# Decode attention beside an MLP on one core: the K and V loads of a unit, cut in two and issued from two queues

## The chip, the cores and the metric

The kernel runs on one core of a Trainium2 chip. The metric is the time of one execution on the device in microseconds (us), as the median of three runs. Beside the timed runs there is one profiled execution, whose trace is what the text reads. Of the engines, PE multiplies matrices, DVE works on vectors, ACT computes activations, POOL does odd jobs, and SP only issues transfers. A transfer is issued as an instruction of an engine's own stream (here SP's or ACT's), waits there for what it needs, and then goes into that engine's queue. The bytes are moved by 16 DMA engines, on which each queue has its share of every transfer.

## The reference, cut to what matters

Two batches, one query token each, 32 heads of 128, a cache of 16384 keys and values per head, all in bf16:

```
q = (x @ wq)                      # x: 2 x 1 x 1024, wq: 1024 x 4096
p = softmax(q . k_cache^T * 128**-0.5)     # k_cache: 2 x 32 x 16384 x 128
a = (p . v_cache) @ wo            # v_cache as k_cache, wo: 4096 x 1024
x1 = x + shifted(gelu(layernorm(x) @ w1)) @ w2
b = x1 + gelu(layernorm(x1) @ w3) @ w4
g = sigmoid(sum(x * gate_w))
out = g * a + (1 - g) * b
```

With one token, the shift of the mixer brings in nothing but zeros. K and V together are 537 MB of some 573 MB read.

## The kernel before, in words

**Units.** The work of attention is cut into 32 units (L88): 16 pairs of heads by 2 batches. The K of a unit is 8.39 MB, laid on 128 partitions as rows of 256 x 128 bf16, so 64 KB in a partition; its V likewise. `cache_rows` (L90) gives that view of the cache, in which each row is contiguous.

**Memory.** One tile `mem` (L80) has five cells of 32 KB per partition. K of an even unit lies in cells 0 and 1, of an odd unit in cells 1 and 2 (`k_cell`, L85): two units in a row share cell 1. V lies in cells 3 and 4 (`v_cell`, L86), but V of unit 30 in 0 and 1. The weights borrow cells: wq lies in 3 and 4 at the start (L124), w1 and w2 in 2, w3 and w4 in 3 and 4 after that (L254 to L257). Whoever loads a cell waits until its last readers are done.

**Loads.** `load_k` and `load_v` (L96, L99) are one transfer each, from SP. `load_v_half` (L102) loads half a row and is used for V of unit 0 alone; `load_v_pieces` (L109) loads V of unit 31 in nine pieces. The weights, x and wo come from SP too (L125, L127, L226, L428, L436). ACT issues nothing but half of the output at the end (L680).

**A unit n** (the loop from L630):
1. `score_first(n)`: four chunks of the half of K that lies in cell 1. DVE transposes a chunk (L462, 2.3 us), then PE does eight matmuls of it into S (L468).
2. `load_k(n + 1)`, which has to wait until cell 1 is free, so for the fourth of these transposes.
3. `score_second(n)`: the other four chunks.
4. `softmax_a(n)`: a transpose (L489) and a maximum (L491) on DVE, a scaled identity `Dm` on ACT (L493).
5. `pv(n - 2)`: 64 matmuls of the V of two units ago (L543).
6. `load_v(n - 1)`, into the cells that these matmuls have read.
7. `pv_end(n - 2)` on DVE and PE, with `wo_project` (L441) in every second unit.
8. `softmax_b(n)`: a matmul (L499), a minimum on DVE (L505), two Exp on ACT (L507). `softmax_c(n)`: a matmul (L521) and a reciprocal (L523).

In unit 31 the V of unit 30 takes the place of step 2 (L635), and the nine pieces of V of unit 31 that of step 6 (L662). In every fourth unit `load_wo_pair` (L428) brings 1 MB of wo from SP. Units 0 and 1 have the MLP's second half (L640 to L656) in place of steps 5 to 7. Before the loop stand the q projection (L268), the gate, the layer norms and the MLP's first half (L623 to L628).

**Order.** Each engine runs its instructions in one order, and that of the source decides except where the framework puts an instruction forward: at 66.20 us matmuls of w3 (L233) run between those of the scores. Semaphore waits are added by the framework, which knows parts of a tile apart. ACT's instructions per unit are `Dm` and then the two Exp, nothing else.

The lines that the diff is about:

```
    def load_k(u):
        nc.sync.dma_start(out=region(k_cell[u], NJ * Dh), in_=cache_rows(A_k_cache, u))

    def load_v(u):
        nc.sync.dma_start(out=region(v_cell[u], NJ * Dh), in_=cache_rows(A_v_cache, u))
```

Of the kernel before, what the change touches and what calls it, by code (L numbers as in the profile page):

```python
# [23 lines left out]
def kernel(  # L24
# [15 lines left out]
    nc = tc.nc  # L40
    P = nc.NUM_PARTITIONS
    B, Sq, D = A_x.shape
    _, H, Sk, Dh = A_k_cache.shape
# [11 lines left out]
    NJ = 2 * Sk // P  # L55
# [6 lines left out]
    CELL = NJ * Dh // 2  # L62
# [19 lines left out]
    def region(cell, elements):  # L82
        return mem[:, cell * CELL : cell * CELL + elements]

    k_cell = [0 if u % 2 == 0 else 1 for u in range(NU)]  # L85
    v_cell = [3] * NU  # L86
# [3 lines left out]
    def cache_rows(cache, u):  # L90
        hp, b = units[u]
        return cache[b, 2 * hp : 2 * hp + 2].rearrange("h s d -> (h s) d").rearrange(
            "(p j) d -> p (j d)", p=P
        )

    def load_k(u):  # L96
        nc.sync.dma_start(out=region(k_cell[u], NJ * Dh), in_=cache_rows(A_k_cache, u))

    def load_v(u):  # L99
        nc.sync.dma_start(out=region(v_cell[u], NJ * Dh), in_=cache_rows(A_v_cache, u))  # L100

    def load_v_half(u, k):  # L102
        at = slice(k * CELL, (k + 1) * CELL)
# [17 lines left out]
    def v_view(u):  # L121
# [12 lines left out]
        out=ident_s[:], in0=ident_f[:], scalar1=-scale, scalar2=None, op0=ALU.mult  # L134
# [8 lines left out]
    for v in range(4):  # L143
        w, e = divmod(v, 2)
        nc.gpsimd.affine_select(
            out=sel[:, v],
            in_=sel[:, v],
# [9 lines left out]
        out=mask4[:], in_=mask4[:], compare_op=ALU.is_ge, fill=0.0,  # L157
# [3 lines left out]
        out=mask4[:], in_=mask4[:], compare_op=ALU.is_ge, fill=0.0,  # L161
# [10 lines left out]
        out=lmat[:].rearrange("p (g h k) -> p g h k", h=2, k=4),  # L172
        in_=hm2[:].unsqueeze(1).unsqueeze(3).to_broadcast([P, P // 8, 2, 4]),
# [4 lines left out]
        out=sel8[:],  # L178
        in_=ident_f[:].rearrange("p (c k) -> p k c", k=QP)[:, 0:8, :],
# [8 lines left out]
        out=hsel[:], in_=sel8[:].rearrange("p (h k) -> p h k", k=4), axis=AX.X, op=ALU.add  # L188
# [69 lines left out]
    lin1.load()  # L258
    lin2.load()
    load_k(0)  # L260

    xT = const.tile([P, KC, B], BF16)
# [27 lines left out]
    for e in range(2):  # L290
        rows = slice(e * HALF, (e + 1) * HALF)
        nc.vector.tensor_copy(
            out=qd[rows],
            in_=qdps[rows].rearrange("p v (hp e b) -> p hp e b v", e=2, b=B)[:, :, e],
# [335 lines left out]
    for n in range(NU):  # L630
        score_first(n)
        if n + 1 < NU:
            load_k(n + 1)
        else:
            load_v(NU - 2)  # L635
        score_second(n)
        softmax_a(n)
        if n == 0:
            load_wo_pair(0)
            lin3.compute(0, 0, FC // 2)  # L640
            softmax_b(n)
            lin3.compute(0, FC // 2, FC)
            lin4.load(0)
            softmax_c(n)
            lin3.compute(1, 0, FC)
            lin4.load(1)
            gelu_T(lin3.acc[:], h2T[:], FC)
        elif n == 1:
            lin4.compute(0, 0, KC // 2)
            softmax_b(n)  # L650
            lin4.compute(0, KC // 2, KC)
            load_v_half(0, 0)
            softmax_c(n)
            lin4.compute(1, 0, KC)
            load_v_half(0, 1)
            mlp_post4()  # L656
        else:
            pv(n - 2)
            if n < NU - 1:
                load_v(n - 1)  # L660
            else:
                load_v_pieces(NU - 1)  # L662
            pv_end(n - 2)
            if n == NU - 1:
                load_wo_last()
            softmax_b(n)
            softmax_c(n)
# [11 lines left out]
    for b, queue in ((0, nc.sync), (1, nc.scalar)):  # L679
        queue.dma_start(  # L680
            out=out[b, 0].rearrange("(k n) -> k n", k=Q4),
            in_=out_row[b : b + QP * (Q4 - 1) + 1 : QP, :],
# [31 lines left out]
```

## Time and profile before

| what | value |
|---|---|
| median of three runs | 1341.24 us (1341.04 to 1341.56) |
| the profiled execution | 1341.09 us |
| its span | 1339.4 us |
| PE, DVE, ACT busy | 768.8, 705.1, 105.2 us (57%, 53%, 8%) |
| bytes moved | 573.33 MB in 14486 packets, 428 GB/s on average |
| rate in the first, the middle and the last of 40 slices | 406, 435 or so, 309 GB/s |
| loads of K, from issue to landing | 28.2 us (25.8 to 30.8) |
| loads of V, from issue to landing | 33.2 us (17.3 to 35.9) |
| SP waiting with a K load in hand (L97) for DVE's transposes of cell 1 | 329.4 us in 31 waits |
| SP waiting with a V load in hand (L100) for PE's pv | 157.9 us in 29 waits |
| DVE waiting for K | 219.5 us in 30 waits |

The span runs from the first to the last instruction, and the time of an execution has 1.7 us more. The busy time of PE, DVE and ACT says how much of the span each works; what matters is who is waited for last. A wait of SP costs nothing as long as the DMA engines have other transfers in their queues; the page's row "DMA" tells how full these are. Queues go by number: q1 is SP's, q10 is ACT's, q8 brings instructions. A packet is one contiguous run of bytes on one DMA engine, here a row in one partition. Landing times are as the semaphores show them. All times on a timeline count from the span's start.

### The profile page before, as it was taken

Reading aid. Unit: us, or ns where it says so; the run is one execution under the profiler, and the core shown is the slowest. Engines: PE = TensorE matmul, PEld = TensorE weight load, DVE = VectorE, ACT = ScalarE, POOL = GpSimd, SP = SyncE. Lnnn points to the kernel's source line nnn. Section 1 sums busy time; section 2 is a strip of 40 time slices with the busy share of each in tenths; the row PEclk is TensorE's granted clock in tenths of the full one; section 3 lists DMA queues with packets and bytes.
Section 4 is the critical chain, followed back from the end, with each engine's and each line's share of the span. In section 5 each row is a group of like instructions: output and inputs, shape, how many; then the busy total and the mean of one; then the engine's idle time right before and its main releaser. Section 6 shows DMA issues by size and latency. Waiting matters only on the chain.

```text
span 1339.4 us, 12490 instructions
## 1 busy us (share of the span) xinstructions
PE 768.8 (57%) x5502; PEld 351.9 (26%) x5502; DVE 705.1 (53%) x695; ACT 105.2 (8%) x165; POOL 15.2 (1%) x54
## 2 busy tenths in 40 slices
PE   2688566554566645556654546665455665555564
PEld 2456222222222212222222212222122222222222
DVE  1445566554556554556655445656444665545561
ACT  0011000000000000000000000000000000000000
POOL 1000000000000000000000000000000000000000
PEclk9977887776788777788877778877678886777886
DMA  9999999999999999999999999999999999999997
GB/s 406 425 429 432 440 431 433 435 423 440 429 435 437 429 429 437 425 435 435 435 431 429 429 437 431 429 427 430 440 431 431 427 433 423 437 435 435 433 423 309
DMA packets 14486, 573.33 MB, mean 428 GB/s; under 512 B 1880, under 2 KB 1888, under 8 KB 4448
## 3 DMA queue, kind: packets, MB, share of 16 engines
q1 hardware_dynamic: 14424, 572.54, 99.3%
q8 instruction: 43, 0.70, 0.2%
q14 instruction: 11, 0.09, 0.0%
q10 hardware_dynamic: 8, 0.00, 0.0%
HBM read 572.53 MB, written 0.00 MB: 427 GB/s over the span
## 4 chain that ended last, share of the span: by engine, by line
DMA 67%; PE 16%; DVE 12%; issue 4%; ACT 0%; another core or an unknown queue 0%; POOL 0%; SPq 0%; ACTq 0%; DVEq 0%
DMA mem<-in_A_k_cache_dram 62%; PE S L468 12%; DVE KT L462 12%; PE misc L233 2%; DMA mem<-in_A_v_cache_dram 2%; DMA xin<-in_A_x_dram 2%; DMA wo<-in_A_wo_dram 1%; PE misc L268 1%; ACT pt L507 0%; PE arow L402 0%; PE oacc L543 0%; DVE St L489 0%; POOL ln_rstd L350 0%; PE misc L344 0%
## 5 line engine op out<-in xcount | busy, mean ns | idle before, releaser
L468 PE MATMUL S<-KT,qw 128*128 128x512 bf16 x2048 | 544.2, 415 | 369.5 <-DVE KT L462 369.3
L462 DVE STREAM_TRANSPOSE KT<-mem 128x2048 f32<-128x2048 f32 x256 | 570.9, 2283 | 271.7 <-DMA mem<-in_A_k_cache_dram 219.5
L468 PEld LDWEIGHTS <-qw 128*128 128x128 bf16 x2048 | 217.7, 107 | 688.3 <-issue 509.2
L543 PE MATMUL oacc<-mem,pt 128*8 128x512 bf16 x2008 | 116.9, 384 | 8.7 <-DMA mem<-in_A_v_cache_dram 8.7
L507 ACT ACTIVATE pt<-St,nb 64x256 bf16<-64x256 f32 x64 | 90.0, 1406 | 149.5 <-DVE nb L505 148.6
L493 ACT ACTIVATE Dm<-ident_s,m 128x128 f32<-128x128 f32 x32 | 12.8, 401 | 998.8 <-DVE m L491 998.8
L521 PE MATMUL misc<-rs,lmat 128*128 128x1 f32 x62 | 18.2, 362 | 85.8 <-ACT pt L507 85.6
L543 PEld LDWEIGHTS <-pt 128*8 128x8 bf16 x2008 | 46.4, 87 | 76.2 <-issue 25.9
L489 DVE STREAM_TRANSPOSE St<-S 128x512 f32<-128x512 f32 x32 | 22.9, 717 | 66.6 <-PE S L468 66.6
L523 DVE RECIPROCAL rinv<-misc 128x1 f32<-128x1 f32 x31 | 5.2, 169 | 96.3 <-PE misc L521 96.3
L559 DVE TENSOR_SCALAR part<-oacc,maskr 128x128 f32<-128x128 f32 x31 | 10.9, 351 | 83.0 <-PE oacc L543 83.0
L590 PE MATMUL misc<-hsel,red 128*128 128x2 f32 x112 | 17.5, 261 | 51.5 <-DVE red L565 51.5
L521 PEld LDWEIGHTS misc<-rs,lmat 128*128 128x128 f32 x62 | 15.5, 310 | 94.2 <-ACT pt L507 94.2
L233 PEld LDWEIGHTS <-mem 128*128 128x128 bf16 x576 | 36.9, 169 | 2.2 <-issue 1.4
L590 PEld LDWEIGHTS misc<-hsel,red 128*128 128x128 f32 x112 | 15.9, 202 | 64.8 <-issue 62.6
L507 ACT ACTIVATION_READ_ACCUMULATOR pt<-St,nb 64x1 f32 x64 | 30.7, 480 | 0.0
L565 DVE SCALAR_TENSOR_TENSOR part<-oacc,maskr,part 128x128 f32<-128x128 f32 x62 | 21.8, 351 | 2.2
L268 PE MATMUL misc<-xT,mem 128*128 128x2 bf16 x256 | 7.1, 165 | 26.1 <-DVE xT L263 23.5
L301 POOL TENSOR_TENSOR qw<-qd,mask 128x16 bf16<-128x16 bf16 x32 | 8.4, 264 | 1188.1 <-PE S L468 1159.5
L599 DVE CAST OT<-misc 64x2 bf16<-64x2 f32 x56 | 9.0, 160 | 22.9 <-PE misc L590 22.6
L499 PE MATMUL misc<-Dm,ones_f 128*128 128x128 f32 x64 | 16.5, 343 | 3.5 <-ACT Dm L493 3.5
L505 DVE TENSOR_REDUCE nb<-misc 64x1 f32<-64x64 f32 x64 | 14.2, 222 | 5.5 <-PE misc L499 3.5
(97 smaller groups left out, 150.7 us busy)
## 6 DMA issues: line engine op xcount, KB each, us to landing
mem<-in_B_w_dram SPq DMA_DIRECT2D x4, 3584.0 KB, 18.8
mem<-in_A_v_cache_dram SPq DMA_DIRECT2D x2, 4096.0 KB
wo<-in_A_wo_dram SPq DMA_DIRECT2D x7, 1024.0 KB, 32.4
mem<-in_A_v_cache_dram SPq DMA_DIRECT2D x7, 1024.0 KB, 24.7
mem<-in_B_w_dram SPq DMA_DIRECT2D x2, 2048.0 KB, 28.6
mem<-in_A_v_cache_dram SPq DMA_DIRECT2D x2, 512.0 KB, 17.9
wo<-in_A_wo_dram SPq DMA_DIRECT2D x4, 256.0 KB, 12.8
mem<-in_A_k_cache_dram SPq DMA_DIRECT2D x32, 28.2
```

The costliest lines, as they stand in the source:

```text
L233: nc.tensor.matmul(ps[:, c - c0, :], lhsT=wc[:, r, :].rearrange("p (m c) -> p c m", c=self.C)[:, c, :], rhs=self.actT[:, k * self.rows + r ...
L268: nc.tensor.matmul(qps[:, h, :], lhsT=wq_t[:, r, h * Dh : (h + 1) * Dh], rhs=xT[:, r, :], start=(r == 0), stop=(r == KC - 1),)
L462: nc.vector.transpose(out=kt[:], in_=Kc.rearrange("p j d -> p (j d)").bitcast(FP32))
L468: nc.tensor.matmul(S, lhsT=t[:, v, NG - 1 - m : NG - 1 - m + P], rhs=ktb[:, half * GT : (half + 1) * GT, w, :, e], start=(first and n == 0 ...
L489: nc.vector.transpose(out=st[:].rearrange("p j r -> p (j r)"), in_=S[:])
L499: nc.tensor.matmul(R_ps[:], lhsT=ones_f[:], rhs=Dm[:], start=True, stop=True)
L505: nc.vector.tensor_reduce(out=nb[rows], in_=R_ps[rows, rows], axis=AX.X, op=ALU.min)
L507: nc.scalar.activation(out=Pt[rows, :, e, :].rearrange("p (m a) k -> p a k m", a=GT // 4), in_=st[rows, :, 0:NG].rearrange("p (a k) m -> p ...
L521: nc.tensor.matmul(tot_ps[:, 0:1], lhsT=lmat[:], rhs=rs[:], start=True, stop=True)
L543: nc.tensor.matmul(acc[QP * q : QP * q + 8, :], lhsT=pts[u % NP][:, g].rearrange("p h k -> p (h k)"), rhs=v_view(u)[:, 4 * g : 4 * g + 4, ...
L565: nc.vector.scalar_tensor_tensor(out=red[:] if twice else part[:], in0=in0.unsqueeze(1).to_broadcast([P, 2, Dh]) if twice else in0, scalar ...
L590: nc.tensor.matmul(ot[:, r, :], lhsT=red[:, r : 2 * Dh : 2], rhs=hsel[:], start=True, stop=True,)
```

## The change

`load_k` and `load_v` call a new function, which cuts each row in the middle and makes two transfers of 128 rows of 32 KB. The first half of every row goes by SP's queue, the second by ACT's. In the cells' terms, the first half is the lower cell of the region and the second the upper. The issue on ACT stands in ACT's stream at the place of the call. `load_v_half` and `load_v_pieces` stay as they are.

```
+    def load_halves(cell, cache, u):
+
+        for k, queue in enumerate((nc.sync, nc.scalar)):
+            at = slice(k * CELL, (k + 1) * CELL)
+            queue.dma_start(out=region(cell, NJ * Dh)[:, at], in_=cache_rows(cache, u)[:, at])
+
     def load_k(u):
-        nc.sync.dma_start(out=region(k_cell[u], NJ * Dh), in_=cache_rows(A_k_cache, u))
+        load_halves(k_cell[u], A_k_cache, u)
 
     def load_v(u):
-        nc.sync.dma_start(out=region(v_cell[u], NJ * Dh), in_=cache_rows(A_v_cache, u))
+        load_halves(v_cell[u], A_v_cache, u)
```

## The prediction

> **What bounds the kernel now.** I read the page's slices first, then its DMA queues, then the stretches of the steady part, then the timeline of one unit, because each says whether the one before it can be taken at its word. The page's two DMA rows and two of its queue rows:
>
> ```profile
> DMA  9999999999999999999999999999999999999997
> GB/s 406 425 429 432 440 431 433 435 423 440 429 435 437 429 429 437 425 435 435 435 431 429 429 437 431 429 427 430 440 431 431 427 433 423 437 435 435 433 423 309
> ...
> q1 hardware_dynamic: 14424, 572.54, 99.3%
> q8 instruction: 43, 0.70, 0.2%
> ```
>
> The DMA row is full in 39 slices of 40, and nearly all bytes go through q1, the queue that SP feeds. No engine's row on the page is above 57% of the span. The stretches (columns: length, busy time and count of five engines, TensorE clock, DMA share, GB/s) say the same more sharply:
>
> ```profile
> 0.00:40.00 40.00, 10.97 (x299) 10.75 (x300) 5.10 (x29) 1.46 (x2) 6.56 (x23) 1.00 0.99 417
> 40.00:80.00 40.00, 28.14 (x230) 17.72 (x230) 22.07 (x27) 0.62 (x2) 0.95 (x2) 1.00 0.99 424
> 80.00:120.00 40.00, 33.18 (x326) 23.25 (x325) 21.64 (x24) 5.22 (x9) 0.26 (x1) 0.78 1.02 435
> ...
> 880.00:1040.00 160.00, 90.15 (x560) 37.86 (x560) 88.23 (x81) 12.83 (x20) 1.06 (x4) 0.77 1.00 431
> ```
>
> A share of 1.00 at 431 GB/s leaves nothing idle. Beyond the start, the time is bytes divided by rate. The chain of waits (DMA 67%, PE 16%, DVE 12%) seems to name a loop through PE and DVE as well; the timeline shows that this loop has room:
>
> ```profile
> 414.31 0.33 SPq L97 DMA_DIRECT2D mem<-in_A_k_cache_dram  x1
> ...
> 428.61 0.33 SPq L100 DMA_DIRECT2D mem<-in_A_v_cache_dram  x1
> ...
> 434.02 0.47 ACT L507 ACTIVATION_READ_ACCUMULATOR pt<-St,nb 64x1 f32 x1
> ...
> 444.03 4.50 DVE L462 STREAM_TRANSPOSE KT<-mem 128x2048 f32<-128x2048 f32 x2 [8.37 <-DMA mem<-in_A_k_cache_dram]
> ...
> 454.54 0.33 SPq L97 DMA_DIRECT2D mem<-in_A_k_cache_dram  x1
> ...
> 468.84 0.33 SPq L100 DMA_DIRECT2D mem<-in_A_v_cache_dram  x1
> ```
>
> K(10) is issued at 414.31 and has landed at 444.03, 29.7 us later, though its 8.39 MB need 19.4 us: until about 424 the queue still works on V(7). So each K is issued some 10 us before the transfers run dry, and each V some 15 us before. The reader should see that PE and DVE may come 10 us late in a unit and the end doesn't move.
>
> **The change part by part.**
>
> *What goes over the wires.* 32 K loads and 30 V loads (V(0) and V(31) are cut already) become 124 halves. Bytes are the same. The trace's DMA packets show what a row costs one of the 16 DMA engines: 64 KB, 8064 rows, median 2.420 us; 32 KB (V(0) alone), 256 rows, 1.215; 16 KB, 0.611; 4 KB, 0.160; a completion's 4 bytes, 0.009. From 32 to 64 KB a row grows by 1.205, so 0.010 us of each row is fixed. Each DMA engine has 8 rows of a transfer (128 over 16), 62 x 8 = 496 in all, and each now costs 2 x 1.215 = 2.430 instead of 2.420: 496 x 0.010 = **+5.0 us**. The 62 added completions cost 62 x 0.009 = **+0.6 us**. Nothing hides either, since the DMA engines are the bound.
>
> *Two queues at once.* The trace of before has hardly two big streams side by side. The nearest row is the instruction fetch on q8: 43 packets of 16 KB, median 1.07 us each instead of the 0.611 of such a row alone, while the 64 KB row beside it took about 2.92 instead of 2.42. So two queues share an engine inside a row, and the pair took 2.92, no more than 2.42 + 0.61 = 3.03. Sharing as such looks free. Bounds: at best one queue's data fills the other's 0.010 us per row, and the +5.0 becomes about -5.0 (62 x 16 half rows at 1.205); at worst each switch costs what a new row costs, and a 64 KB row goes at the price of 16 KB rows (4 x 0.611 = 2.444, 496 x 0.024 = +11.9) or of 4 KB rows (16 x 0.160 = 2.560, +69). I take the 32 KB row, the nearest in size and destination.
>
> The Trainium skill (DMA: Bandwidth & Descriptors, Queues, rings and completion order) says that an engine drains a whole packet from one queue before it switches. The q8 rows disagree: a 16 KB fetch beside a long row would take 0.61 us, not 1.07. The sum is the same by either.
>
> The same page (Anatomy of one DMA) puts about 2.0 us of fixed cost on every DMA, fitted on GpSimd's path; that speaks against this change. Paid in the open it would make +124 us of 62 added transfers, about 1465 us. The trace's V(0) halves follow each other with no gap (last row of the first begun at 136.59, first row of the second at 136.64), so a full queue hides it.
>
> *When the halves start.* They aren't issued together in effect. The two regions of K overlap in cell 1, which is freed by the first four transposes of the unit before; the other cell is free much earlier. The early half goes at once: for even K behind the V load on SP (near 469 instead of 495.78 for K(12)), for odd K behind the Exp pair on ACT (near 434.5 instead of 454.54 for K(11)). The late half goes when the whole load went before. From then on both queues nearly always hold work, and two halves side by side take 2 x 9.7 = 19.4 us, as the whole did. Is there still cover? Let K land at 0. The queue without the late half holds a V half and the next early half, 19.4 us of work, and by 10.5 (444.03 to 454.54) at most 10.5 us of it is done. Then 9.7 us are added: at least 18.6 us for the 14.3 until the next V (454.54 to 468.84). About 4 us is left in the worst case, more if the other V half is still under way. V lands later against its use (L543), perhaps by some us, within that cover. Cost 0.
>
> *ACT.* 62 issues, 0.33 us each on SP (the output's took 1.35 on ACT). Behind a waiting K half stands Dm (L493), which needs all eight transposes, so comes later anyway; behind a waiting V half stands Exp (L507), which needs matmuls that PE runs after the pv that V waits for (428.61, Exp at 431.66). Cost 0; if the cover fails, an Exp is late by about 1 us in a unit with 4 us to spare. SP loses nothing: one issue stays where one was.
>
> *The start.* Here something does move. K(0)'s second half needs no wait, so ACT issues it at once, beside wq. Four pieces of the chain at the start, and two of SP's issues:
>
> ```profile
> 1.24 21.99 DMA xin<-in_A_x_dram
> ...
> 23.48 6.09 PE misc L268 x223
> ...
> 48.99 0.70 POOL ln_rstd L350
> ...
> 49.90 3.53 another core or an unknown queue
> ```
>
> ```profile
> 102.99 0.33 SPq L97 DMA_DIRECT2D mem<-in_A_k_cache_dram  x1
> 121.31 7.77 SPq L104 DMA_DIRECT2D mem<-in_A_v_cache_dram  x2
> ```
>
> wq and x, now at half rate until the half is done, land 8 x 1.215 = 9.7 us later. The chain from 23.48 to 49.7 (q, layer norms, w1, w2) shifts with them to 59.4, where before the first scores began at 53.45, after K(0). So everything that PE paces is late by 5.9 us: SP's V(0) issue at 121.31 goes at 127.3, and ACT's early half of K(3), behind the Exp of unit 1 that ended at 121.4, too. What was queued before it: wq 8.39, w1 and w2 4.19, K(0) to K(2) 25.17, w3 and w4 14.68, wo 1.05, together 53.5 MB. 40 x (417 + 424 + 435) is 51.0 MB at 120 us, and the other 2.4 MB at 432 GB/s are done at 125.6, with the longer rows 125.9. V(0) was in time by 4 us; now the queues are dry from 125.9 until 127.3, and 1.0 us more until a first packet (wq: issue 0.79, packet 1.8): **+2.4 us**. Bounds: 0, if 1.5 us of the lag is made up; about +5, if more is added on the way.
>
> *The end.* V(30)'s early half goes ahead of V(29)'s use; the bytes and the order of V(31)'s pieces stay. Cost 0, give or take 1.
>
> **Sum.** 5.0 + 0.6 + 2.4 = +8.0 us. The profiled execution took 1341.09, 1.7 more than its span; the median of the runs is 1341.24. Forecast **1349.2 us**, 0.6% slower. A measurement tells 0.2%, 2.7 us, from no change.
>
> **The rivals.**
>
> *A, not slower: two queues fill each other's gaps.* Place: every row change. Price: the rows at their slope, -5.0, with the start's +2.4: 1341.2 - 2.6 = 1338.6. For it: a pair with q8 took 0.11 us less than the two alone, and the rate per row grows with its size as if only gaps cost. Against: the fetch doesn't go where K goes, and 4 bytes hold an engine for 0.009 us too. It decides from the point at which half of the fixed 0.010 is filled.
>
> *B, sharing costs: switching between two long streams breaks the rows up.* By the 16 KB row, 11.9 + 0.6 + 2.4 = +14.9, 1356.1. For it: no row of before shows two streams into these tiles. Against: the pair with q8.
>
> *C, the change does less than it says: the transfers run dry in each unit,* because V lands late, holds back the next V, and the cover of 4 us is gone. From there each us is paid about 29 times: 1 us a unit gives 1378. Against it: an early half stands in one of the queues nearly always.
>
> **How the numbers follow.** Forecast's case (1344 to 1353) 0.50; A (1335 to 1344) 0.26; B (1353 to 1365) 0.18; C 0.06. Faster by over 0.2% is half of A, 0.13; within is the rest of A and the lower edge of the forecast's, 0.16; slower 0.71. The range leaves out the ends of A and B and C: 1337 to 1358.
>
> **What would show it.** Packets go from 14486 to about 23,400 (62 x 144 more), with 260 MB on ACT's queue. The steady stretches stay at a share of 1.00, with about 0.4% less GB/s: 430 for 431; if they rise to 433 or more, A is right, and below 427, B. The first scores begin near 59, and the slices around 126 us show a dip. Waits of L543 for V may grow without cost. A DMA share under 0.98 in the steady part would be C. I'm wrong altogether if ACT's halves don't get the places in its order that I gave them.

## The result, and the profile after

The changed kernel takes 1355.19 us (1354.15 to 1356.32, four runs), beside 1341.14 for the kernel before on the same chip: 14.0 us more, a ratio of 1.0104 (95% interval 1.0089 to 1.012). It is slower, as forecast, and by 14.0 instead of 8.0 us. The span of its profiled execution is 1353.4 us, 14.0 longer too.

The page of the changed kernel, the rows that answer to those of before, with its count of packets:

```profile
DMA  9999899999999999999999999999999999999997
GB/s 401 431 388 426 372 433 433 434 429 429 430 431 432 427 433 430 424 433 431 432 427 430 433 430 433 430 423 432 429 431 431 430 425 435 430 425 430 427 432 303
DMA packets 23415, 573.35 MB, mean 424 GB/s; under 512 B 2872, under 2 KB 2880, under 8 KB 5440
...
q1 hardware_dynamic: 14424, 312.49, 54.1%
q10 hardware_dynamic: 8936, 260.05, 44.7%
```

The packets are those of the forecast (23,415 for 23,400), and so are the bytes on ACT's queue. The row GB/s has what the forecast lacked: two deep slices, 388 and 372, the third and the fifth, where before had 429 and 440. The stretches of the changed kernel (columns as before), and last, for comparison, the kernel before from 120 to 160 us:

```profile
0.00:40.00 40.00, 2.34 (x88) 2.44 (x89) 7.52 (x20) 1.28 (x1) 5.41 (x20) 1.00 0.96 404
40.00:80.00 40.00, 31.52 (x368) 20.79 (x366) 16.61 (x32) 0.39 (x2) 1.84 (x4) 0.83 1.01 433
80.00:120.00 40.00, 33.41 (x330) 24.03 (x329) 20.81 (x23) 3.58 (x6) 0.26 (x1) 0.74 0.94 391
120.00:160.00 40.00, 32.20 (x280) 19.60 (x280) 21.10 (x20) 3.40 (x5) 0.26 (x1) 0.74 0.91 386
880.00:1040.00 160.00, 98.80 (x581) 37.60 (x574) 89.39 (x82) 12.93 (x20) 1.05 (x4) 0.79 1.00 429
...
120.00:160.00 40.00, 32.29 (x336) 19.75 (x335) 22.73 (x26) 4.56 (x7) 0.26 (x1) 0.80 0.99 427
```

The fifth line is the steady part: a share of 1.00, and 429 GB/s where before had 431. The first four have moved 40 x (404 + 433 + 391 + 386) = 64.6 MB; before had moved 40 x (417 + 424 + 435 + 427) = 68.1 by then. The missing 3.6 MB are 8 us at 432 GB/s. So the loss has at least two places, and the greater one is over after 160 us.

A sum over the trace's packets, divided by the 16 engines, says it again: the time in which a DMA engine works grew from 1332.7 to 1340.3 us, and the rest of the span from 6.7 to 13.0. Dry time of 2.7 us lies between 90 and 95 us and 3.8 between 150 and 155, and after the last load come 2.2 us more than before (6.7 instead of 4.4), in which nothing is loaded. (The three make 8.7 and not 6.3, since the sum counts a moment with two packets on one engine twice. Laid end to end, each packet begins 3 to 4 ns before the one ahead of it ends, and the 558 more packets on an engine make some 2 us of that.)

What happened at the start can be read in the timeline. First DVE and SP near the first dry stretch, and last the same issue of SP in the kernel before:

```profile
33.05 4.50 DVE L468 STREAM_TRANSPOSE KT<-mem 128x2048 f32<-128x2048 f32 x2 [29.30 <-DMA mem<-in_A_k_cache_dram]
37.47 0.13 DVE L269 COPY xT<-xin 128x16 bf16<-128x16 bf16 x1
...
92.25 7.89 SPq L232 DMA_DIRECT2D mem<-in_B_w_dram  x2
...
83.35 7.85 SPq L226 DMA_DIRECT2D mem<-in_B_w_dram  x2
```

Then SP and PE near the second, and last the same matmuls of PE in the kernel before:

```profile
130.24 23.28 SPq L110 DMA_DIRECT2D mem<-in_A_v_cache_dram  x2
...
146.30 6.85 PE L239 MATMUL misc<-h2T,mem 128*128 128x2 bf16 x112
...
153.62 0.37 SPq L100 DMA_DIRECT2D mem<-in_A_k_cache_dram  x1
...
121.86 6.86 PE L233 MATMUL misc<-h2T,mem 128*128 128x2 bf16 x112
```

And these two stretches of the changed kernel in numbers:

```profile
90.00:95.00 5.00, 5.00 (x77) 5.00 (x76) 0.64 (x3) 2.03 (x4) 0.00 (x0) 0.50 0.53 183
...
150.00:155.00 5.00, 5.00 (x58) 3.71 (x58) 1.81 (x2) 0.00 (x0) 0.00 (x0) 0.66 0.44 128
```

In the first fence, DVE transposes two chunks of K(0) *before* it copies x (L269 here, L263 before). K(0)'s second half shared the engines with wq, and both landed near 33 (wq at 23.1 before). So x, which PE needs for q, was copied at 37.5 instead of 23.3. w4's load, which waits for PE to be done with w3, goes at 92.25 instead of 83.35, and by then the queues have run out: 183 GB/s from 90 to 95. In the second fence SP's merged entry holds two issues, the first half of V(0) at 130.24 and the second at 153.2. Between them SP waits for the last part of the MLP's matmuls, which PE starts only at 146.30, after four of the eight chunks of unit 2's scores; before, it started at 121.86, ahead of them. Behind that waiting issue stands K(3)'s first half, at 153.62. From 150 to 155 the rate is 128 GB/s.

### The profile page after: what moved, and what is told of

The parts are those of the page before. It is cut to its first block, busy times and chain, and to the rows that moved or that the text cites. A ratio compares the mean times of both kernels' runs of the same rounds, so it can differ in the third digit from the quotient of the medians.

```text
span 1353.4 us, 12604 instructions
## 1 busy us (share of the span) xinstructions
PE 825.2 (61%) x5502; PEld 346.4 (26%) x5502; DVE 704.9 (52%) x695; ACT 106.0 (8%) x165; POOL 15.2 (1%) x54
## 2 busy tenths in 40 slices
DMA packets 23415, 573.35 MB, mean 424 GB/s; under 512 B 2872, under 2 KB 2880, under 8 KB 5440
## 4 chain that ended last, share of the span: by engine, by line
DMA 62%; PE 31%; DVE 4%; issue 1%; another core or an unknown queue 1%; ACT 0%; POOL 0%; SPq 0%; DVEq 0%
DMA mem<-in_A_v_cache_dram 52%; PE S L474 21%; DMA mem<-in_A_k_cache_dram 10%; PE oacc L549 6%; DVE KT L468 3%; PE misc L239 2%; PE misc L274 1%; PE misc L618 0%; PE misc L527 0%; ACT pt L513 0%; DVE part L571 0%; PE misc L505 0%; DVE red L571 0%; PE arow L447 0%
## 5 line engine op out<-in xcount | busy, mean ns | idle before, releaser
L468 DVE STREAM_TRANSPOSE KT<-mem 128x2048 f32<-128x2048 f32 x256 | 579.8, 2294 | 407.1 <-PE S L474 221.2
L474 PE MATMUL S<-KT,qw 128*128 128x512 bf16 x2048 | 591.6, 439 | 249.8 <-DVE KT L468 237.8
L474 PEld LDWEIGHTS <-qw 128*128 128x128 bf16 x2048 | 211.8, 110 | 557.0 <-issue 417.5
L549 PE MATMUL oacc<-mem,pt 128*8 128x512 bf16 x2008 | 155.8, 403 | 180.9 <-DMA mem<-in_A_v_cache_dram 180.9
L239 PEld LDWEIGHTS <-mem 128*128 128x128 bf16 x576 | 37.0, 167 | 1.4 <-issue 0.5
L511 DVE TENSOR_REDUCE nb<-misc 64x1 f32<-64x64 f32 x64 | 14.2, 222 | 22.6 <-PE misc L505 21.1
L505 PE MATMUL misc<-Dm,ones_f 128*128 128x128 f32 x64 | 20.5, 413 | 2.8 <-ACT Dm L499 2.8
L274 PEld LDWEIGHTS <-mem 128*128 128x128 bf16 x256 | 7.1, 104 | 39.6 <-DMA mem<-in_A_wq_dram 32.9
L505 PEld LDWEIGHTS misc<-Dm,ones_f 128*128 128x128 f32 x64 | 13.3, 259 | 7.6 <-issue 4.3
L571 DVE SCALAR_TENSOR_TENSOR red<-oacc,maskr,part 128x256 f32<-128x256 f32 x31 | 14.7, 473 | 0.8
```

What stands on the lines that cost most here:

```text
L239: nc.tensor.matmul(ps[:, c - c0, :], lhsT=wc[:, r, :].rearrange("p (m c) -> p c m", c=self.C)[:, c, :], rhs=self.actT[:, k * self.rows + r ...
L274: nc.tensor.matmul(qps[:, h, :], lhsT=wq_t[:, r, h * Dh : (h + 1) * Dh], rhs=xT[:, r, :], start=(r == 0), stop=(r == KC - 1),)
L468: nc.vector.transpose(out=kt[:], in_=Kc.rearrange("p j d -> p (j d)").bitcast(FP32))
L474: nc.tensor.matmul(S, lhsT=t[:, v, NG - 1 - m : NG - 1 - m + P], rhs=ktb[:, half * GT : (half + 1) * GT, w, :, e], start=(first and n == 0 ...
L505: nc.tensor.matmul(R_ps[:], lhsT=ones_f[:], rhs=Dm[:], start=True, stop=True)
L511: nc.vector.tensor_reduce(out=nb[rows], in_=R_ps[rows, rows], axis=AX.X, op=ALU.min)
```

## The experiments

All times are medians of four to seven runs, with runs of the kernel before on the same chip, 1341.1 us. Where a cut of code names `load_whole`, that is a new function which loads whole rows in one transfer, from SP or from the queue that it is given. Two theories stood against each other at first.

**Theory 1.** The added rows and completions cost their fixed part all the way, some 5 us, and the rest is lost where the queues run dry at the start.

**Rival 1.** Two queues at once cost rate by switching, all the way: the prediction's rival B, whose 1356.1 the measured time nearly met.

**e2, both halves from SP.** It has the rows of the change and one queue.

```
-        for k, queue in enumerate((nc.sync, nc.scalar)):
+        for k, queue in enumerate((nc.sync, nc.sync)):
```

> Both halves from SP's queue, one behind the other; the same rows and completions as in the changed kernel, one queue, and DVE's order as before. Theory 1: the rows alone, 1341.2 + 5.6 = 1346.8 (1345 to 1349), steady rate 430 GB/s as in the changed kernel, nothing lost in the first 160 us. Rival 1 (switching between queues is what costs): rate back near 432 and a time within 3 us of before. Rival 2 (landing as two transfers delays the scores whatever the queue): near 1355.

1345.88 us, 4.7 more than before (1.0035, 1.0023 to 1.0048). A stretch of its start, and then one of the steady part for e2, the changed kernel and the kernel before:

```profile
80.00:120.00 40.00, 34.24 (x327) 23.86 (x328) 21.78 (x24) 4.98 (x8) 0.27 (x1) 0.75 1.01 430
...
600.00:800.00 200.00, 121.51 (x703) 48.97 (x703) 112.93 (x102) 16.05 (x25) 1.32 (x5) 0.76 1.00 430
...
600.00:800.00 200.00, 120.23 (x703) 45.81 (x702) 107.95 (x99) 16.12 (x25) 1.32 (x5) 0.79 1.00 430
...
600.00:800.00 200.00, 110.32 (x696) 46.48 (x696) 108.63 (x100) 16.04 (x25) 1.32 (x5) 0.78 1.00 432
```

Without ACT's queue, the rate in the steady part is the changed kernel's own (in five stretches of 200 us, from 200 to 1200, both have 429 to 431 GB/s, before 431 to 433), and the start is whole. So the steady loss belongs to the rows and the transfers that come with them, and two thirds of the 14.0 do not. The order of the instructions is whole too: x is copied at 22.99, and the last part of the MLP starts at 122.11, so the new order came with the second queue. Rival 2 of the expectation, a landing in two parts, would have cost as much with one queue, and is out.

**e5, quarters from SP.** Four transfers of 16 KB rows for each load, all from SP.

```
-        for k, queue in enumerate((nc.sync, nc.scalar)):
-            at = slice(k * CELL, (k + 1) * CELL)
+        for k in range(4):
+            at = slice(k * CELL // 2, (k + 1) * CELL // 2)
...
```

> Four transfers of 16 KB rows instead of two of 32 KB, all from SP's queue. Theory 1 (each row and each completion costs its fixed part): three added rows instead of one, 3 x 4.7 = +14 us by the run with halves from SP, +14.6 by the packet rows (496 x 0.026 + 186 x 0.009): 1355 (1353 to 1357), rate 427 GB/s. Rival (what the halves cost is not the rows but one thing per load, a landing or an issue): no more than 7 us over before.

1354.79 us, 13.7 more (1.0101, 1.0087 to 1.0115). The steady stretch:

```profile
880.00:1040.00 160.00, 96.09 (x559) 38.24 (x558) 85.22 (x80) 12.83 (x20) 1.05 (x4) 0.76 1.01 427
```

Three added cuts of each row cost 13.7, one costs 4.7: 4.6 each. The cost goes with the number of cuts and isn't one thing per load, as a fixed part of each row would have it. It is a little below 5.6, the prediction's term for rows and completions. Rows and transfers were added together, so the times don't tell their prices apart; the packets do, with a median of 1.216 us for a row of 32 KB in e2, 2.420 for one of 64 KB before, and 0.009 for a completion.

**e4, whole rows, K from SP and V from ACT.** The edit is shown against the kernel before.

```
     def load_k(u):
-        nc.sync.dma_start(out=region(k_cell[u], NJ * Dh), in_=cache_rows(A_k_cache, u))
+        load_whole(k_cell[u], A_k_cache, u)
...
     def load_v(u):
-        nc.sync.dma_start(out=region(v_cell[u], NJ * Dh), in_=cache_rows(A_v_cache, u))
+        load_whole(v_cell[u], A_v_cache, u, nc.scalar)
```

> Rows stay whole: K whole from SP, V of units 1 to 30 whole from ACT. Two queues, no added rows or completions, start as before. Theory 1: 1341 to 1343, steady rate as before (432). Rival 1 (switching costs): at least 5 us more than before, and a steady rate of 430 or less. If two queues fill each other's gaps (the rival A of the prediction): 1336.

1387.87 us, 46.7 more (1.0343, 1.0329 to 1.0357). Theory 1 missed this by far, and by the time alone Rival 1 would have won; the timeline says otherwise. K(3), V(1) and the landing of K(3):

```profile
139.33 55.94 SPq L97 DMA_DIRECT2D mem<-in_A_k_cache_dram  x2
...
152.92 0.39 ACTq L97 DMA_DIRECT2D mem<-in_A_v_cache_dram  x1
...
183.63 4.50 DVE L466 STREAM_TRANSPOSE KT<-mem 128x2048 f32<-128x2048 f32 x2 [27.49 <-DMA mem<-in_A_k_cache_dram]
```

```profile
180.00:190.00 10.00, 4.01 (x11) 1.69 (x11) 5.12 (x5) 0.00 (x0) 0.00 (x0) 0.50 0.41 177
190.00:200.00 10.00, 10.00 (x57) 3.35 (x55) 9.24 (x5) 0.00 (x0) 0.00 (x0) 0.91 0.54 210
```

K(3) is issued at 139.33 and V(1) from ACT at 152.92. From then on V(1), which is needed one unit later, has half the engines. K(3) lands at 183.63, 44 us after its issue, where a K load of before took 28. DVE waits 27.5 us; the next K can't be issued until its four transposes are done, and meanwhile V(1) is through as well and both queues are empty: 177 and 210 GB/s. This is e4's longest dry stretch, from 186.5 to 195.9; in every second unit or so after it comes one of some 1 us, and one of 3.4 near the end. Rows were not slower: the packets of 64 KB have a median of 2.420 us on SP's queue and 2.418 on ACT's, 2.420 before. So switching costs a row nothing, and two queues do harm by taking the order away. This is the prediction's rival C at work, in another kernel: the halves of the change mostly avoid it in the steady part, since each queue carries half of everything.

That left the start. **Theory 1** says three things: at the start K(0)'s half beside wq is one cause, what comes after it another, and the end is separate.

**e3, K(0) alone in halves.** All else is whole and from SP.

```
     def load_k(u):
-        load_halves(k_cell[u], A_k_cache, u)
+        if u == 0:
+            load_halves(k_cell[u], A_k_cache, u)
+        else:
+            load_whole(k_cell[u], A_k_cache, u)
...
-        load_halves(v_cell[u], A_v_cache, u)
+        load_whole(v_cell[u], A_v_cache, u)
```

> Only K(0) is cut, its second half from ACT beside wq; all else whole from SP as before. Theory 1: the steady part is that of before (432 GB/s), and the start loses what the late wq makes it lose, with the first transposes ahead of x in DVE's order: a dry stretch near 90 to 100 us, +2 to +5 us, 1343 to 1346. Rival 1 (switching all the way): no more than 1 us over before.

1345.92 us, 4.8 more (1.004, 1.0027 to 1.0052), with one load of 62 cut. The stretch that lost most:

```profile
80.00:120.00 40.00, 33.32 (x321) 23.48 (x320) 21.69 (x23) 3.59 (x6) 0.26 (x1) 0.74 0.86 348
```

The start is dry between 80 and 120, and the steady part is back at 433 GB/s (880 to 1040). (The profiled run is the longest of the five, 1348.07, so the stretch shows more than the median lost.) One half-load issued too early costs as much as the rows of all 62.

**e1, K(0) whole, the others in halves.**

```
     def load_k(u):
-        load_halves(k_cell[u], A_k_cache, u)
+        if u == 0:
+            load_whole(k_cell[u], A_k_cache, u)
+        else:
+            load_halves(k_cell[u], A_k_cache, u)
```

> K(0) goes whole from SP as before, all other K and V in halves from two queues. Theory 1 (0.010 us for each added row and 0.009 for each completion, 5.6 us, and the rest, about 8 us, lost to dry queues in the first 160 us): wq and x land at 23 us again, and what the first 100 us lost comes back; what is lost around 150 us, where V(0)'s second half and K(3)'s first wait for the last part of the MLP, may stay, as the scores of unit 2 still stand ahead of that in DVE's order: 1348 to 1351. Rival 1 (the two queues cost rate by switching all the way): within 2 us of the changed kernel, 1353 to 1356, with the same rate in the steady part.

1353.78 us, 12.6 more (1.0094, 1.008 to 1.0107): only 1.4 us better than the change, outside what Theory 1 said, and within Rival 1's. So K(0) isn't the only culprit at the start. Its packets have 3.7 us of dry time between 80 and 160 us, where the changed kernel's have 6.5, so a part of the start did come back. By the timeline the other culprit is this:

```profile
71.65 2.05 PEld L245 LDWEIGHTS <-mem 128*128 128x128 bf16 x31 [3.70 <-DMA mem<-in_B_w_dram]
...
90.30 7.86 SPq L238 DMA_DIRECT2D mem<-in_B_w_dram  x2
```

At 71.65 PE waits for w3 (`mem<-in_B_w_dram`), which it never did in the kernel before: K(1)'s early half, issued by ACT at 45.66 when w1 and w2 had been used, shared the engines with K(0) and w3 in SP's queue. Scores go on late behind it, and w4's load goes at 90.30. With K(0) whole, the same lag comes by another early half. In the changed kernel the two don't add up, presumably since the second finds PE late already. No run leaves K(1) alone whole, so this is read from the timeline; e6 shows that with all early loads whole the start is that of before. One more thing in this trace costs time, and in the steady part: near 884 us both queues are empty for about 1 us (352 GB/s from 880 to 890).

**e8, only the start in halves** (K of units 0 to 3, V of unit 1).

```
-        load_halves(k_cell[u], A_k_cache, u)
+        if u < 4:
+            load_halves(k_cell[u], A_k_cache, u)
+        else:
+            load_whole(k_cell[u], A_k_cache, u)
...
+        if u < 2:
...
```

> Halves from two queues for K of units 0 to 3 and V of unit 1 alone; the rest whole from SP. Theory 1: the dry stretches of the changed kernel near 90 and 150 us come back, 6.5 us, and the rows add 0.4: 1346.5 to 1349. Rival (the start's gaps are made good later, as the transfers catch up): under 1344.

1348.54 us, 7.4 more (1.0055, 1.0042 to 1.0067). Both dry stretches are there, and the steady part is that of before (the profiled run is again the longest of the five, 1350.06):

```profile
80.00:120.00 40.00, 33.42 (x327) 23.91 (x326) 20.86 (x23) 3.58 (x6) 0.26 (x1) 0.74 0.93 387
120.00:160.00 40.00, 32.51 (x280) 19.72 (x279) 21.20 (x20) 3.39 (x5) 0.26 (x1) 0.74 0.92 388
880.00:1040.00 160.00, 90.64 (x562) 38.21 (x563) 87.31 (x82) 12.83 (x20) 1.06 (x4) 0.77 1.00 433
```

Nothing of the loss is made good later, since a full queue has nothing to catch up with. Five of its loads are cut, 0.4 us by e2's measure, so the start is worth 7.0.

**e7, only units in the middle in halves** (K of units 4 to 27, V of units 2 to 25). The edit is e8's with `4 <= u < 28` and `2 <= u < 26`.

> Halves from two queues for K of units 4 to 27 and V of units 2 to 25 alone; start and end whole from SP. Theory 1: the rows alone, 4.7 x 48/62 = 3.6: 1344 to 1346, and the end as in before, 4.5 us from the last load to the end of the span. Rival (two queues cost something in every unit): 1348 or more.

1344.74 us, 3.6 more (1.0029, 1.0018 to 1.004). 48 of 62 loads at e2's measure are 3.6. In 24 units with two queues nothing else is lost that the time shows.

**e6, from there to the end** (K from unit 4, V from unit 2). The edit is e8's with `u >= 4` and `u >= 2`.

> K from unit 4 and V from unit 2 on in halves from two queues, everything before that whole from SP. Theory 1 (rows, the start, and some 2 us at the end): the start is that of before, so 4.7 x 57/62 for the rows and 2 for a later end: 1347 to 1348.5, no dry stretch before 160 us. Rival (the two queues lose the time in the steady part): 1352 or more.

1347.99 us, 6.9 more (1.005, 1.0038 to 1.0063). It has nine more cut loads than e7, 0.7 us, and costs 3.3 more: the end is worth 2.6. (The runs of the two don't overlap: 1347.3 to 1348.5 and 1344.6 to 1346.2.) The end of e7, where V(30) is whole and from SP, and that of the changed kernel:

```profile
1288.84 0.33 SPq L97 DMA_DIRECT2D mem<-in_A_v_cache_dram  x1
...
1305.90 1.40 ACT L522 ACTIVATE pt<-St,nb 64x256 bf16<-64x256 f32 x1 [4.59 <-DVE nb L520]
...
1316.55 6.09 PE L558 MATMUL oacc<-mem,pt 128*8 128x512 bf16 x80 [6.91 <-DMA mem<-in_A_v_cache_dram]
```

```profile
1301.65 0.33 ACTq L100 DMA_DIRECT2D mem<-in_A_v_cache_dram  x1
...
1327.07 0.58 PE L549 MATMUL oacc<-mem,pt 128*8 128x512 bf16 x1 [9.66 <-DMA mem<-in_A_v_cache_dram]
...
1333.06 1.40 ACT L513 ACTIVATE pt<-St,nb 64x256 bf16<-64x256 f32 x1 [16.57 <-DVE nb L511]
...
1344.40 4.41 PE L618 MATMUL misc<-pt,mem 128*128 128x2 bf16 x160
```

In e7 the Exp of unit 31 run at 1305.90, before V(30) is there at 1316.55, and the last matmuls are done while the last loads arrive; its end is the last piece of wo and four matmuls, at 1339.06. In the changed kernel V(30)'s second half is issued at 1301.65 and PE gets to V(30) at 1327.07. The Exp of unit 31 come after that, at 1333.06, because PE's order now has some matmuls of V(30) ahead of the one that the Exp need. So all 160 matmuls of V(31) are left at 1344.40 and take 4.4 us, where in e7 they ran piece by piece as the data came. The last row of V(31) ends only at 1346.7, so PE's late start alone is worth about 1 us, an estimate from the last 16 matmuls, which take 0.6 us in e7. A second thing has changed: SP issues the last four pieces of wo at 1242.3, and no longer behind V(31)'s pieces (1317.9 before, 1321.5 in e7). So V(31) is what arrives last, and behind it more work is left than behind wo.

The parts close: start 7.4 (e8), middle 3.6 (e7), end 3.3 (e6 less e7), each with its rows, together 14.3, and the change measured 14.0.

No version here beats the kernel before. Every cut of a row costs, and the one thing a second queue could give, filling idle engines, has no room at a share of 1.00.

## Why the prediction was right and wrong

*The bound* was read rightly. The DMA engines set the end, so anything that lengthens their work or leaves them dry is paid in full, and until the last loads nothing else is: PE and DVE waited in quite different places after the change (PE for V 181 us in all, before 9), which cost nothing by itself.

*The rows* (+5.0 and +0.6) were right, at 4.7 by e2 and 4.6 for each cut by e5. A fixed 0.010 us in a row of 2.42, seen in the packets of before, was enough to see it coming. The sum left out that packets overlap by 3 to 4 ns: e2's packets add up to 6.4 us more for an engine than those of before, and less 2.0 of overlap that is 4.4.

*Two queues at once* came out as taken, free of cost, but the reading behind it was wrong. From the instruction fetch I concluded that an engine shares itself inside a row. The fetch doesn't run beside the long row: in 42 of 43 cases the lengthened row begins 3 to 16 ns before the fetch ends, so the two follow each other. The pair of a fetch and a row of 64 KB takes 1.07 and 2.92, some 0.95 us more than the two alone (3.03), and not 0.11 less, which rival A had for it. Why both grow is left open. With both queues full, rows of 32 KB take a median of 1.215 us on SP's queue and 1.216 on ACT's, as alone; had they been mixed, each would have taken about twice that. The trace doesn't name a packet's engine, but the packets can be strung into 16 chains by their times, and there four of five successive rows between 200 and 1200 us change the queue. So here an engine takes one row whole and then the other queue's. This agrees with what I set aside: the Trainium skill (DMA: Bandwidth & Descriptors, Queues, rings and completion order) says that a whole packet is drained from one queue before the engine switches. The halves' sum didn't depend on it.

*Rival B* met the time within 1 us for a wrong reason. e2 and e7 rule it out. A total that fits is no proof of the mechanism; only the stretches and the runs told the two apart.

*The halves' start* and its cover were right in the steady part: in e7's packets no stretch over 0.1 us is to be found between the start and the end in which more than half of the engines stand idle. The cover is thin all the same: e1 ran dry once, near 884 us, which is rival C in a single unit.

*The start* is the step that failed: +2.4 forecast, 7.0 measured (e8). The lag was in the text, and half of its consequences. Three things were missing. The lag was priced at V(0)'s issue alone, though w4's load comes earlier, waits for PE too, and had no more cover: its issue was late by 8.9 us, and 2.7 us of dry queue are there. I assumed the instructions' order of before, but with the second queue the framework put two transposes ahead of x, then scores ahead of the MLP's last part; this made the lag 14.2 instead of 9.7 us at x, and V(0)'s second half late by 24 us. And SP's order makes a late issue hold back all behind it, here K(3)'s first half: 3.8 us. My upper bound for this term, +5, was too low as well. Of the signs that I gave, the dip near 126 us didn't come (it came at 90 and at 150), and the first scores began at 48.7, not near 59.

*The end* (0, give or take 1) failed too, at 2.6 (e6 against e7). The bytes were the same, as I said, but their order was not: in the changed kernel V(30)'s early half was in SP's queue from 1278 us on, while K(31) was still to land at 1290.6 (before: 1272.9, with V(30) issued at 1283.5), and the last of wo went ahead of V(31). Which of these made the end late, and by how much, is argued from the order; e6 and e7 show only that the cuts at the end do.

In sum: 4.7 for 5.6, 7.0 for 2.4, 2.6 for 0. The sign held, and the size was short by the two ends of the kernel. That the range held is in part luck: 1355.2 lies outside the band of the forecast's own case (1344 to 1353) and in that of B, whose mechanism was not at work.

## What to carry to other kernels

When the transfers are full, a second queue brings no rate; it takes away the order in which things arrive, and a load that nobody needs yet then has half the engines while one that PE waits for comes late (e3: one half-load, 4.8 us; e4: 46.7 us). The Trainium skill says as much of the rate in its rules for kernel authors (DMA: Bandwidth & Descriptors), where it finds no bandwidth in spreading transfers over issuing engines; the cost of the lost order is what these runs add. Look for such a change's price at the start and the end, where cover is thin, and price every issue that the lag reaches, with the new order of the instructions in mind, not the nearest one alone.

## What the runs showed of the hardware that was not expected

A row keeps its length beside a second full queue: 1.215 and 1.216 us for 32 KB, 2.420 and 2.418 for 64 KB (e4), and the chains of packets mostly change the queue after each row, so sharing goes row by row. An instruction fetch of 16 KB takes its engine for 1.07 us, against 0.61 for a row of that size, and the row behind it takes 0.5 us longer (the kernel before). The fixed part of a row stays, whether the next row is of the same queue or of the other: e7's 24 units on two queues pay the same per load (3.6 us for 48) as e2's on one (4.7 for 62).
